# Retention and channel-mix kernel: the values of blocks 1 to 5 computed in 64x64 quarters of the PE array, by couples of head pairs

## The chip, the cores and the metric

The kernel runs on one core of one Trainium2 chip. The metric is the device time of one execution in microseconds (us), lower is better; a time quoted for a kernel is the median of three runs. The engines are named as the profile names them: PE (TensorE), with PEld for its weight loads, DVE (VectorE), ACT (ScalarE), POOL (GpSimd) and SP (SyncE, which here only issues DMAs).

## What is computed

The reference is a retention layer (attention with a decay per head and a running state) followed by a channel-mix layer, all in float32:

```python
# q, k, v: (B=4, H=8, S=768, D=64); lam: (8,)
for b in range(nb):                       # nb = 12 blocks of 64 positions
    intra = (qb @ kb.T * Dmask) @ vb      # Dmask[i, j] = lam ** (i - j) for i >= j
    inter = (qb * lam ** (pos + 1)) @ kv_state
    out[b] = intra + inter
    kv_state = lam ** 64 * kv_state + (kb * lam ** (63 - pos)).T @ vb
x = out as (B, S, 512); x_prev = x shifted by one position
xk = mu_k * x + (1 - mu_k) * x_prev;  xr the same with mu_r
k = relu(xk @ w_k);  v = (k * k) @ w_v;  r = sigmoid(xr @ w_r)
return r * v                              # w_k 512x1024, w_v 1024x512, w_r 512x512
```

## The kernel before

The sequence is cut into six blocks of 128 positions (n = 0 to 5). Every block goes through the same stages. Eight heads make four head pairs, `hp` = 0 to 3; the two heads of a pair (`ab` = 0, 1) lie on the two halves of the 128 partitions. A block has an even and an odd half of 64 positions (`eo` = 0, 1).

- Loads. `load_hp` (L) brings the keys in both layouts, `load_qv` (N) the queries and values. SP issues them. The four input tiles and the `kin` tile have one buffer each, which the next block reuses.
- `scores` (A): keys times queries into the PSUM tile `sc`. For n > 0 each multiplication is 64x64: rows are the head, columns the half. `decay` (a) multiplies the scores on DVE by a table `Dt` of powers of lam into `mv`; `decay_queries` (q) writes the queries times powers of lam into the other 64 partitions of the same `mv`.
- `decay_keys` (k) scales the keys on ACT, `sums` (U) forms keys times values in PSUM tile `u`, `even_state` and `odd_state` (u, w) carry the state `st` forward on DVE. `to_values` copies the state by ACT into the 64 partitions of the value tile that the values leave free.
- `values` (B): one matmul of 128 rows (64 of scores with values, 64 of queries with the state) and 64 columns for each half, batch and head, into PSUM tile `xp`.
- `mix_prev` (e, E), `mix` (f, F) and `split_x` (y, x) form xk and xr and split each into a high and a low part; then the three weight products `r_part` (R, Q), `k_part` (K; in block 0 `k_product`, G) and `v_part` (V), each as three passes of 128x128 by 512 matmuls in a rounded float32 type, with `k_square` (h), `k_split` (p), `r_out` (s) and `v_out` (o) around them.

In block 0 the state is zero, the stages differ in form, and the weights are brought in and converted (S, c, C, D). An unscaled float32 matmul call (scores, sums, values) appears in the trace as two instructions, a rounded one as one.

What sets the order is the string `ORDER`: each three-character step issues its instructions in this sequence on every engine, SP's queue too, and `InOrder` (line 28) keeps the engines from changing it. Waits come from data and from buffers: PSUM has one `sc` pair of banks, one `u` and one `xp` bank, and four banks under the tag `m`, which the weight products, the values and other tiles share. The pool `work` has two `mv` buffers.

The lines that matter here: 114 to 132 (loads), 266 to 350 (scores to `to_values`), 366 to 379 (`values`), 508 on (`ORDER`). The values before:

```python
for eo in range(1 if n == 0 else 2):
    for b in range(B):
        for ab in range(2):
            rows = slice(ab * 64, ab * 64 + 64)
            ...
            tensor.matmul(xp[rows, b, eo, :], vs[eo][:, b, ab, :], mv[:, eo, b, ab, :], start=True, stop=True)
```

Of the kernel before, what the change touches and what calls it, by code (L numbers as in the profile page):

```python
# [18 lines left out]
HP = H // 2  # L19
# [17 lines left out]
def tile_retention_moe(  # L37
# [46 lines left out]
    VS, Q, KT, KN = {}, {}, {}, {}  # L84
# [29 lines left out]
    def load_hp(n, hp):  # L114
        if n == 0:
            return load_first(hp, 0)
        if not KIN:
            KIN.append(const.tile([128, 2, 2, 512], F32, tag="kin", name="kin"))
        t = KIN[0][:, hp % 2]
        views((n, hp), [None, None, None, t[:, 0], t[:, 1]])  # L120
        sync.dma_start(t.rearrange("p c o -> p (c o)"), kk[n - 1, hp])

    def load_qv(n, hp):
        if n == 0:
            return load_first(hp, 1)
        if hp not in QV:
            QV[hp] = const.tile([128, 3, 512], F32, tag=("qv0", "qv1", "wst", "top")[hp], name=f"qv{hp}")
        t = QV[hp]
        views((n, hp), [t[:, 0], t[:, 1], t[:, 2], None, None])
# [4 lines left out]
    smalls = tiny.tile([128, 52 + H], F32, name="smalls")  # L134
# [3 lines left out]
    lows, impulse, ecol, lrow, erow, prow, mus, pair, parity = (smalls[:, a:b] for a, b in (  # L138
        (0, 8), (8, 33), (33, 36), (36, 44), (44, 45), (45, 46), (46, 54), (54, 58), (58, 60)))
# [5 lines left out]
    KD = tiny.tile([128, H], F32, name="KD")  # L145
# [13 lines left out]
    gpsimd.tensor_tensor(KD, lrow, erow.broadcast_to([128, H]), op=ALU.pow)  # L159
# [104 lines left out]
    scs, mvs, us, xps, ts = {}, {}, {}, {}, {}  # L264

    def scores(n, hp):
        q, kt = Q[n, hp], KT[n, hp]
        if n == 0:
            if hp == 1:
# [11 lines left out]
        if (n, hp) not in scs:  # L281
            pair = ps_s.tile([128, 2, 2, B, 64], F32, tag="sc", name="sc")
            scs.update({(n, hp // 2 * 2 + i): pair[:, :, i] for i in range(2)})
        for b in range(B):
            for eo in range(2):
                for ab in range(2):
                    rows = slice(ab * 64, ab * 64 + 64)
                    tensor.matmul(scs[n, hp][eo * 64:eo * 64 + 64, ab, b], kt[rows, b, eo, :], q[rows, b, eo, :],
                                  start=True, stop=True)

    def mv_of(n, hp):
        if (n, hp) not in mvs:
            mvs[n, hp] = work.tile([128, 2, B, 2, 64], F32, tag="mv", name="mv")
        return mvs[n, hp]

    def decay(n, hp):
        sc, mv = scs.pop((n, hp)), mv_of(n, hp)
        if n == 0:
# [3 lines left out]
            return  # L302
        for eo in range(2):
            rows = slice(eo * 64, eo * 64 + 64)

            i = slice(64 - eo * 64, 128 - eo * 64)
            vector.tensor_tensor(
                mv[rows, eo], sc[rows].rearrange("p a b i -> p b a i"),
                Dt[rows, 2 * hp:2 * hp + 2, i].rearrange("p (o a) i -> p o a i", o=1).broadcast_to([64, B, 2, 64]),
                op=ALU.mult)  # L310

    def decay_queries(n, hp):
        q, mv = Q[n, hp], mv_of(n, hp)
        for eo in range(2):
            dr = slice(64, 128) if eo == 0 else slice(0, 64)
            for ab in range(2):
                rows = slice(ab * 64, ab * 64 + 64)
                lp = LP[rows, hp:hp + 1, :].broadcast_to([64, B, 64])
                vector.tensor_tensor(mv[dr, eo, :, ab, :], q[rows, :, eo, :], lp, op=ALU.mult)

    def decay_keys(n, hp):
        kn = KN[n, hp]
        for ab in range(2):
            h = 2 * hp + ab
            scalar.activation(kn[:, :, ab, :], kn[:, :, ab, :], AF.Copy, scale=(PW if n == 0 else KD)[:, h:h + 1])

    def sums(n, hp):
# [8 lines left out]
        if (n, hp, 0) not in us:  # L336
            for eo in halves:
                pair = ps_1.tile([128, 2, B, 64], F32, tag=("u", "xp")[eo], name="u")
                us.update({(n, hp // 2 * 2 + i, eo): pair[:, i] for i in range(2)})
        for b in range(B):  # L340
            for ab in range(2):
                for eo in halves:
                    rows = slice(eo * 64, eo * 64 + 64)
                    tensor.matmul(us[n, hp, eo][ab * 64:ab * 64 + 64, b], kn[rows, b, ab, :], vs[eo][rows, b, ab, :],
                                  start=True, stop=True)


    def to_values(n, hp, eo, x):
        for ab in range(2):
            scalar.copy(VS[n, hp][eo][64 - eo * 64:128 - eo * 64, :, ab, :], x[ab * 64:ab * 64 + 64])  # L350

# [14 lines left out]
    def values(n, hp):  # L366
        mv, vs = mvs.pop((n, hp)), VS[n, hp]
        pool, tag = (ps_1, ("xp", "u")[hp % 2]) if n == 0 else (ps_m, "m")
        xp = pool.tile([128, B, 2, 64], F32, tag=tag, name="xp")
        for eo in range(1 if n == 0 else 2):  # L370
            for b in range(B):
                for ab in range(2):
                    rows = slice(ab * 64, ab * 64 + 64)
                    if n == 0:
                        tensor.matmul(xp[rows, b].rearrange("p e i -> p (e i)"), vs[1][:, b, ab, :], mv[:, ab, b, :], start=True, stop=True)
                    else:
                        tensor.matmul(xp[rows, b, eo, :], vs[eo][:, b, ab, :], mv[:, eo, b, ab, :],
                                      start=True, stop=True)
        xps[n, hp] = xp.rearrange("p b e i -> p b (e i)")

# [101 lines left out]
    def v_out(n, b):  # L482
# [8 lines left out]
        M=lambda n, hp: load_first(hp, 2), b=keep_raw, G=lambda f, hp: k_product(0, f, hp),  # L491
# [17 lines left out]
L00 Z10 L01 M00 M03 T0 k00 Sk4 A00 A01 L02 T2 a00 a01 k03 ck4 M01 B00 A02 Ck4 b00 e00 N01 E00 f00 N02 U00 a02 B01 L03 F00 Dk4  # L509
y00 u00 B02 k01 A03 b01 Sk5 x00 N03 M02 G20 G00 b02 ck5 Sk6 Sk7 E01 a03 G30 Ck5 e01 e02 f01 F01 E02 B03 Dk5 y01 f02 G10 ck6 b03  # L510
U01 Ck6 ck7 k02 Ck7 G11 e03 x01 y02 Sk2 G21 Dk6 G31 f03 U02 u01 Sk3 Dk7 U03 G01 ck2 Ck2 E03 G22 y03 Sr1 ck3 G32 Ck3 G02 G12 G33
Sr0 G23 Sr3 Sv3 Dk2 F02 cr1 Dk3 G13 G03 h03 cr0 Sr2 F03 h02 Cr1 Sv0 h00 cr3 Cr0 N11 Sv1 p01 Dr1 cr2 K07 K05 Dr0 h01 Cr3 Cr2 h05
x02 Dr2 Dr3 x03 K04 p00 h04 u03 Q00 N10 h07 Q01 cv0 Sv2 cv3 u02 q11 Q02 Cv0 Q03 L11 Cv3 Dv0 R00 s03 R01 cv1 Cv1 L10 Dv3 R02 k10
R03 K06 k11 s01 A10 A11 q10 Dv1 cv2 Cv2 U10 L12 p02 h06 U11 Dv2 L13 p03 s02 u11 N13 a10 V04 a11 V02 w11 V03 V05 N12 k13 B11 s00
u10 B10 o01 V00 E11 w10 o02 k12 e11 q13 U13 A12 N20 A13 U12 L20 V06 V01 E10 q12 e10 u12 a12 F11 x11 L21 V07 u13 k20 k21 f10 f11
a13 F10 B13 B12 w13 y10 y11 E13 e13 N21 N22 e12 w12 A20 o03 o00 f12 f13 y12 y13 U21 U20 q21 A21 F13 L22 K10 K11 a20 u20 K13 a21
h11 x13 h10 u21 q20 k22 K14 h13 K12 p10 K15 w20 L23 w21 k23 E12 N23 F12 U22 U23 x10 A23 h12 A22 B20 h15 p11 a23 h14 x12 B21 Q10
E21 L30 e20 L31 Q11 Q12 E20 f20 u22 F20 F21 k31 Q13 s12 s13 q23 K17 h17 K16 N31 e21 N30 R10 h16 R11 R12 p12 u23 w22 x21 k30 p13
x20 V10 V11 f21 R13 w23 s10 a22 V14 V15 q22 o12 B23 E23 B22 y20 U31 U30 A31 A30 s11 y21 e23 L33 o10 V12 N32 u30 f23 y23 e22 V13
V16 F23 u31 f22 q30 x23 E22 F22 y22 o11 V17 K23 h23 o13 w30 x22 K22 K24 L32 q31 Q20 a31 w31 h22 N33 k32 a30 Q21 K25 h24 B31 h25  # L520
B30 k33 U33 q32 N41 e31 E31 F31 A33 U32 A32 f31 Q22 L41 Q23 e30 N40 K26 a32 p22 s22 f30 p21 u33 s23 L40 K20 h26 a33 E30 R20 F30
R21 R22 k40 k41 K21 R23 u32 w32 h20 K27 q33 A40 h21 s21 w33 x30 U41 U40 p20 y30 h27 A41 B33 y31 e33 s20 E33 x31 L43 p23 u40 B32
V22 V24 V25 f33 N43 e32 F33 V23 E32 V20 x33 L42 f32 V21 k42 o21 F32 q40 y32 Q30 a41 w40 o20 x32 a40 Q31 V26 o22 Q32 q41 Q33 s33
y33 V27 K33 k43 N42 o23 u41 K32 w41 K31 s32 h32 B41 B40 h31 N51 A43 e41 h33 E41 U43 f41 e40 p31 A42 L51 F41 a42 E40 U42 K30 h30
a43 R30 L50 K36 R31 q42 h36 R32 f40 k51 u42 F40 u43 K37 R33 s31 h37 K34 s30 K35 k50 q43 B42 x40 p30 h35 p33 h34 w42 N50 N52 B43
A51 y40 U50 U51 p32 y41 A50 E43 x41 e42 V36 V30 L52 V37 F43 e43 N53 f43 a50 o33 f42 V34 x43 V32 y42 V35 E42 o32 V33 a51 q51 y43
# [72 lines left out]
```

## Time and profile before

| | |
|---|---|
| time, median of 3 runs | 396.35 us (395.99 to 396.37) |
| the profiled execution | 395.83 us |
| its span, first to last instruction | 394.0 us |
| PE busy | 387.8 us, 98% of the span |
| DVE, ACT, POOL busy | 244.3, 201.5, 34.4 us |
| granted PE clock | 1.0 of full speed in all 40 slices |

The span lies 1.8 us inside the time of its own execution, and that execution 0.5 us below the median of the runs. Instructions of PE overlap, so the time of a group is read from the chain of waits (start to start), not from its busy time.

### The profile page before, as it was taken

What the parts mean: (1) busy time and instruction counts of PE and PEld (TensorE: products, weight loads), DVE (VectorE), ACT (ScalarE), POOL (GpSimd) and SP (SyncE); (2) the same over time, 40 slices, a digit from 0 to 9 for tenths busy, and PEclk for the clock granted to TensorE, in tenths of its full rate; (3) what the DMA queues carried; (4) which work ended last, traced back from release to release, by engine and by line L of the source; (5) the groups of instructions that cost most, each with busy time, mean ns of one, the idle gap of its engine ahead of it and who ended that gap; (6) DMA issues with size and microseconds to landing.
All of it is one profiled execution on the core that took longest, in us unless ns stands there. A gap on an engine that the chain in (4) does not pass through costs nothing.

```text
span 394.0 us, 8421 instructions
## 1 busy us (share of the span) xinstructions
PE 387.8 (98%) x3532; PEld 321.4 (82%) x3532; DVE 244.3 (62%) x392; ACT 201.5 (51%) x367; POOL 34.4 (9%) x104
## 2 busy tenths in 40 slices
PE   8899999999999999999999999999999999999996
PEld 5777888888888888888888888888888888888886
DVE  6987898699857375876565285855456844222411
ACT  4989997575755362475612347721266542222400
POOL 6540000100110010100100010210000000000000
PEclk9999999999999999999999999999999999999999
DMA  8998934654250081250701070340100001000002
GB/s 302 411 352 300 352 109 137 201 143 166 69 150 0 30 238 57 62 154 0 209 34 57 27 208 8 109 134 27 53 2 2 2 2 55 27 27 2 0 28 80
DMA packets 13606, 42.58 MB, mean 108 GB/s; under 512 B 1920, under 2 KB 2304, under 8 KB 13568
## 3 DMA queue, kind: packets, MB, share of 16 engines
q1 hardware_dynamic: 9824, 35.68, 28.2%
q10 hardware_dynamic: 3744, 6.36, 4.4%
q8 instruction: 28, 0.46, 0.5%
q14 instruction: 10, 0.08, 0.1%
HBM read 35.74 MB, written 6.29 MB: 107 GB/s over the span
## 4 chain that ended last, share of the span: by engine, by line
PE 94%; DVE 1%; POOL 1%; ACT 1%; issue 1%; DMA 0%; POOLq 0%; DVEq 0%
PE vp L33 34%; PE kp L33 32%; PE rp L33 17%; PE xp L33 5%; PE sc L33 3%; PE u L33 3%; POOL lastw L33 1%; PE table L33 0%; DMA smalls<-small 0%; POOL ts L33 0%; ACT ts L33 0%; DVE xl L33 0%; DVE raw L33 0%; POOL pows L33 0%; POOL top L33 0%
## 5 line engine op out<-in xcount | busy, mean ns | idle before, releaser
L33 PE MATMUL vp<-wv,k 128*128 128x512 f32 (+1 forms) x600 | 134.5, 382 | 0.0
L33 PEld LDWEIGHTS vp<-wv,k 128*128 128x128 f32 x600 | 108.9, 188 | 21.9 <-ACT kf L33 0.2
L33 PE MATMUL kp<-xh,wk 128*128 128x512 f32 x384 | 123.3, 391 | 0.0
L33 PEld LDWEIGHTS kp<-xh,wk 128*128 128x128 f32 x384 | 72.1, 188 | 15.7 <-ACT kf L33 0.4
L33 PE MATMUL kp<-xl,wk 128*128 128x512 f32 x192 | 75.0, 390 | 0.0
L33 PE MATMUL rp<-wr,xh 128*128 128x512 f32 x192 | 59.5, 391 | 0.0
L33 DVE TENSOR_TENSOR kf<-kf 128x512 f32<-128x512 f32 x40 | 27.3, 691 | 51.9 <-ACT kf L33 51.7
L33 ACT ACTIVATE kf<-kp 128x512 f32<-128x512 f32 x48 | 28.2, 594 | 54.3 <-PE kp L33 37.8
L33 ACT COPY qv<-st 64x256 f32<-64x256 f32 x80 | 32.4, 405 | 27.4 <-DVE st L33 23.4
L33 DVE TENSOR_TENSOR xl<-ts,xh 128x512 fp32r<-128x512 f32 x48 | 32.5, 688 | 22.0 <-ACT xh L33 21.9
L33 ACT CAST xh<-ts 128x512 fp32r<-128x512 f32 x48 | 29.2, 617 | 28.8 <-DVE rt L33 23.4
L33 PEld LDWEIGHTS kp<-xl,wk 128*128 128x128 f32 x192 | 36.0, 188 | 7.8 <-DVE xl L33 0.6
L33 PEld LDWEIGHTS rp<-wr,xh 128*128 128x128 f32 x192 | 35.8, 188 | 7.5
L33 DVE TENSOR_TENSOR rt<-vp,rt 128x512 f32<-128x512 f32 (+1 forms) x25 | 16.4, 665 | 38.4 <-PE vp L33 38.4
L33 PE MATMUL rp<-wr,xl 128*128 128x512 f32 x96 | 37.4, 390 | 0.0
L33 ACT ACTIVATE ts<-xp,omu 128x512 f32<-128x512 f32 x40 | 26.2, 688 | 18.5 <-PE xp L33 16.9
L33 DVE TENSOR_TENSOR mv<-qv,LP 64x256 f32<-64x256 f32 x80 | 33.6, 421 | 1.5
L33 DVE TENSOR_TENSOR k<-kf,k 128x1024 fp32r<-128x1024 f32 x24 | 29.3, 1225 | 8.1 <-ACT k L33 7.8
L33 DVE SCALAR_TENSOR_TENSOR ts<-xp,smalls,ts 128x512 f32<-128x512 f32 x40 | 29.2, 746 | 7.5 <-ACT ts L33 7.1
L33 DVE TENSOR_TENSOR mv<-sc,Dt 64x512 f32<-64x512 f32 (+1 forms) x48 | 32.5, 686 | 1.1 <-ACT Dt L33 0.5
L33 ACT ACTIVATE rt<-rp 128x512 f32<-128x512 f32 x24 | 14.0, 594 | 30.7 <-PE rp L33 30.7
L33 POOL COPY ts<-lastw 128x4 f32<-128x4 f32 x48 | 15.6, 327 | 138.2 <-DVE xl L33 138.2
(66 smaller groups left out, 294.2 us busy)
## 6 DMA issues: line engine op xcount, KB each, us to landing
qv<-qv SPq DMA_DIRECT2D x40, 256.0 KB, 6.1
kin<-kk SPq DMA_DIRECT2D x20, 512.0 KB, 5.7
out<-rt ACTq DMA_DIRECT2D x23, 256.0 KB, 2.0
raw<-w_v SPq DMA_DIRECT2D x4, 1023.8 KB, 7.2
in<-parts SPq DMA_DIRECT2D x5, 512.0 KB, 5.5
raw<-w_k SPq DMA_DIRECT2D x2, 1023.8 KB, 11.7
raw<-k_half SPq DMA_DIRECT2D x4, 511.8 KB, 8.1
raw<-w_r SPq DMA_DIRECT2D x4, 511.8 KB, 12.2
```

Source lines behind the costliest of these rows:

```text
L33: return lambda *args, **kw: self.tc.keep_in_program_order(op(*args, **kw))
```

## The change

For n > 0 two pairs make a couple (`c` = hp // 2), and the steps L, N, A, a, k, U and B are done for a couple at once. Each pair of a couple gets its own half of the partitions in scores, sums and values. So a score matmul has rows by head and columns by pair, a sum has rows by pair and columns by head, and a value matmul of 128 rows is replaced by two of 64 rows, one of decayed scores with values and one of decayed queries (new tile `qd`) with the state (new tile `SV`), the second added to the first in PSUM. `mv` and `qd` of a couple fill the two `mv` buffers. `Dt` gets a second copy of a table part by POOL (`table`, step d). SP's loads are joined: one DMA of 1 MB where two of 512 KB or four of 256 KB stood. `ORDER` is another order of the steps, the opening included.

```diff
@@ loads
-        t = KIN[0][:, hp % 2]
-        views((n, hp), [None, None, None, t[:, 0], t[:, 1]])
-        sync.dma_start(t.rearrange("p c o -> p (c o)"), kk[n - 1, hp])
+        t = KIN[0].rearrange("p c i o -> p (c i) o")
+        ...
+        sync.dma_start(t.rearrange("p c o -> p (c o)"), kk[n - 1, hp // 2])
...
-            QV[hp] = const.tile([128, 3, 512], F32, tag=("qv0", "qv1", "wst", "top")[hp], name=f"qv{hp}")
-        ...
-        for e in range(2):
-            rows = slice(e * 64, e * 64 + 64)
-            sync.dma_start(t[rows, e:e + 2].rearrange("p c o -> p (c o)"), qv[n - 1, hp, rows])
+            QV[c] = (const.tile([128, 4, 512], F32, tag=("qv0", "wst")[c], name=f"qv{c}"),
+                     const.tile([128, 2, 512], F32, tag=("qv1", "top")[c], name=f"sv{c}"))
+        ...
+        sync.dma_start(t.rearrange("p c o -> p (c o)"), qv[n - 1, c])
@@ scores
-                for ab in range(2):
-                    rows = slice(ab * 64, ab * 64 + 64)
-                    tensor.matmul(scs[n, hp][eo * 64:eo * 64 + 64, ab, b], kt[rows, b, eo, :], q[rows, b, eo, :],
+                for i in range(2):
+                    for ab in range(2):
+                        rows = slice(ab * 64, ab * 64 + 64)
+                        tensor.matmul(sc[i * 64:i * 64 + 64, ab, eo, b], KT[n, hp + i][rows, b, eo, :], Q[n, hp + i][rows, b, eo, :],
@@ table, decay, decay_queries, decay_keys
+    def table(hp):
+        gpsimd.tensor_copy(Dt[64:128, 2 * hp:2 * hp + 2, 64:128], Dt[64:128, 2 * hp + 2:2 * hp + 4, 0:64])
...
         for eo in range(2):
-            rows = slice(eo * 64, eo * 64 + 64)
-            ...
             vector.tensor_tensor(
-                mv[rows, eo], sc[rows].rearrange("p a b i -> p b a i"),
+                mv[:, eo], sc[:, :, eo].rearrange("p a b i -> p b a i"),
...
-                vector.tensor_tensor(mv[dr, eo, :, ab, :], q[rows, :, eo, :], lp, op=ALU.mult)
+            vector.tensor_tensor(qds[n, c][hp % 2 * 64:hp % 2 * 64 + 64, :, :, ab, :], q[rows].rearrange("p b e i -> p e b i"), lp, op=ALU.mult)
...
-            scalar.activation(kn[:, :, ab, :], kn[:, :, ab, :], AF.Copy, scale=(PW if n == 0 else KD)[:, h:h + 1])
+            scale = PW[:, 2 * hp + ab:2 * hp + ab + 1] if n == 0 else KD[:, hp + ab:hp + ab + 1]
+            scalar.activation(kn[:, :, ab, :], kn[:, :, ab, :], AF.Copy, scale=scale)
@@ sums
-            for ab in range(2):
-                for eo in halves:
-                    rows = slice(eo * 64, eo * 64 + 64)
-                    tensor.matmul(us[n, hp, eo][ab * 64:ab * 64 + 64, b], kn[rows, b, ab, :], vs[eo][rows, b, ab, :],
+            for eo in halves:
+                for ab in range(2):
+                    for i, u in enumerate(both):
+                        rows = slice(i * 64, i * 64 + 64)
+                        tensor.matmul(u[ab * 64:ab * 64 + 64, eo, b], kn[rows, eo * B + b, ab, :], vs[eo][rows, b, ab, :],
@@ to_values, values
-            scalar.copy(VS[n, hp][eo][64 - eo * 64:128 - eo * 64, :, ab, :], x[ab * 64:ab * 64 + 64])
+            scalar.copy(SV[n, hp // 2 * 2][eo][i:i + 64, :, ab, :], x[ab * 64:ab * 64 + 64])
...
+        both = [ps_m.tile([128, B, 2, 64], F32, tag="m", name="xp") for _ in range(2)]
+        parts = ((vs, mv), (SV[n, hp], qds[n, hp // 2]))
+        for eo in range(2):
+            for b in range(B):
+                for s, (stay, move) in enumerate(parts):
+                    for ab in range(2):
+                        for i, xp in enumerate(both):
+                            rows = slice(i * 64, i * 64 + 64)
+                            tensor.matmul(xp[ab * 64:ab * 64 + 64, b, eo, :], stay[eo][rows, b, ab, :], move[rows, eo, b, ab, :],
+                                          start=s == 0, stop=s == 1)
@@ ORDER (its first line)
-L00 Z10 L01 M00 M03 T0 k00 Sk4 A00 A01 L02 T2 a00 a01 k03 ck4 M01 B00 A02 Ck4 b00 e00 N01 E00 f00 N02 U00 a02 B01 L03 F00 Dk4
+L00 L01 M03 Z10 T0 A00 A01 k03 T2 M00 Sk4 L02 a00 k00 N01 a01 B00 L03 A02 ck4 b00 B01 Ck4 e00 E00 M02 N02 f00 a02 Sk5 Dk4 y00
```

How the order moves, at three places. First PE in the opening, before (block 0; `sc`, `xp`, `u` are scores, values and sums, `kp` the first weight product):

```order
L33 MATMUL sc<-in 128x128 x8
L33 MATMUL u<-in 64x64 x8
L33 MATMUL xp<-mv,in 64x128 x16
L33 MATMUL sc<-in 128x128 x8
L33 MATMUL kp<-xh_78,wk_265 128x512
```

and in the change, from the same scores of pair 2 on:

```order
L33 MATMUL sc<-in 128x128 x8
L33 MATMUL xp<-mv,in 64x128 x8
L33 MATMUL u<-in 64x64 x8
L33 MATMUL sc<-in 128x128 x8
L33 MATMUL xp<-mv,in 64x128 x8
L33 MATMUL kp<-xh_78,wk_256 128x512
```

The values of pair 1 go ahead of the sums of pair 0, and the values of pair 2 follow the scores of pair 3. Up to the end of the four sums the change issues 18 `kp` matmuls, before 21.

Second, ACT in the opening, before, from the copy of the first values on (`raw<-xp` is that copy, `in` the scaled keys, `st<-u` the copy of a sum):

```order
L33 COPY raw<-xp 128x512
L33 ACTIVATE ts<-raw,omu 128x4x128 x2
L33 CAST wk_265<-raw 128x512
L33 CAST xh_78<-ts 128x512
L33 COPY st_94<-u 128x256
L33 ACTIVATE in<-in,PW 128x4x64 x2
L33 COPY raw<-xp 128x512
L33 CAST xh_82<-ts 128x512
L33 COPY raw<-xp 128x512
L33 ACTIVATE ts<-raw,omu 128x4x128 x4
```

and in the change:

```order
L33 COPY raw<-xp 128x512
L33 ACTIVATE ts<-raw,omu 128x4x128 x2
L33 CAST wk_256<-raw 128x512
L33 CAST xh_78<-ts 128x512
L33 COPY raw<-xp 128x512
L33 COPY st_94<-u 128x256
L33 ACTIVATE ts<-raw,omu 128x4x128 x2
L33 ACTIVATE in<-in,PW 128x4x64 x2
L33 COPY raw<-xp 128x512
L33 CAST xh_82<-ts 128x512
```

After the first cast of `xh` ACT now takes the copy of pair 1's values first, which PE computes after the scores of pair 2. The set of ACT operations up to the first `kf` is the same.

Third, PE at the small matmuls of blocks 1 and 2 that stand ahead of a `vp` or `rp` run, before:

```order
L33 MATMUL u<-qv_817,kin 64x64 x16
L33 MATMUL u<-qv_759,kin 64x64 x16
L33 MATMUL sc<-qv_759,kin 64x64 x16
L33 MATMUL sc<-qv_817,kin 64x64 x16
L33 MATMUL xp<-mv,qv_568 64x64 x16
L33 MATMUL xp<-mv,qv_485 64x64 x16
```

and such a place in the change:

```order
L33 MATMUL sc<-qv_465,kin 64x64 x32
L33 MATMUL u<-qv_465,kin 64x64 x32
L33 MATMUL xp<-mv,qv_812 64x64 x4
L33 MATMUL xp<-qd,sv_813 64x64 x4
L33 MATMUL xp<-mv,qv_812 64x64 x4
L33 MATMUL xp<-qd,sv_813 64x64 x4
```

Sixteen such groups of four make the values of a couple, 64 calls where 32 stood. Counted over blocks 1 to 5, small matmuls break into the weight products 12 times before and 13 times in the change.

## Rows read from the trace of the kernel before

**Rows 1.** The page, busy time by engine and granted clock by slice.

```profile
PE 387.8 (98%) x3532; PEld 321.4 (82%) x3532; DVE 244.3 (62%) x392; ACT 201.5 (51%) x367; POOL 34.4 (9%) x104
PEclk9999999999999999999999999999999999999999
```

**Rows 2.** Chain of waits, opening: start us, us to the next piece, what.

```profile
9.80 0.58 ACT raw L33
...
24.08 0.69 PE u L33 x16
24.76 14.99 PE kp L33 x63
39.76 10.88 PE rp L33 x48
```

**Rows 3.** Chain of waits, blocks 1 to 5.

```profile
53.36 1.09 PE sc L33 x64
54.45 0.93 PE u L33 x64
...
66.55 2.02 PE xp L33 x64
...
103.78 0.93 PE sc L33 x64
104.71 2.02 PE xp L33 x64
106.73 5.69 PE rp L33 x24
112.42 5.44 PE kp L33 x24
...
251.26 0.62 PE sc L33 x32
251.88 0.85 PE u L33 x29
```

**Rows 4.** Chain of waits, the end.

```profile
368.84 22.08 PE vp L33 x120
...
390.95 0.42 DVE rt L33
```

**Rows 5.** Timeline of PE, opening; in brackets the idle time before and what ended it.

```profile
10.98 1.16 PE L33 MATMUL sc<-in 64*128 64x128 f32 x16 [1.27 <-DMA in<-parts]
12.07 0.69 PE L33 MATMUL u<-in 128*64 128x64 f32 x16
24.08 0.69 PE L33 MATMUL u<-in 128*64 128x64 f32 x16 [0.71 <-ACT st L33]
```

**Rows 6.** Timeline of ACT, opening.

```profile
12.16 0.61 ACT L33 CAST xh<-ts 128x512 fp32r<-128x512 f32 x1
23.13 0.62 ACT L33 CAST wk<-raw 128x512 fp32r<-128x512 f32 x1 [1.00 <-DVE raw L33]
23.66 0.37 ACT L33 COPY st<-u 128x256 f32<-128x256 f32 x1
30.64 0.59 ACT L33 ACTIVATE kf<-kp 128x512 f32<-128x512 f32 x1
```

**Rows 7.** Groups by form, DVE and ACT: busy us, mean ns, idle before.

```profile
L33 DVE TENSOR_TENSOR mv<-sc,Dt 64x512 f32<-64x512 f32 x40 | 27.4, 686 | 0.4
L33 DVE TENSOR_TENSOR mv<-qv,LP 64x256 f32<-64x256 f32 x80 | 33.6, 421 | 1.5
L33 ACT ACTIVATE kin<-kin,KD 128x256 f32<-128x256 f32 x40 | 17.9, 503 | 1.8 <-DMA kin<-kk 1.6
```

**Rows 8.** DMA issues: what, how many, KB each, median us to landing.

```profile
kin<-kk SPq DMA_DIRECT2D x20, 512.0 KB, 5.7
raw<-w_v SPq DMA_DIRECT2D x4, 1023.8 KB, 7.2
raw<-w_r SPq DMA_DIRECT2D x4, 511.8 KB, 12.2
```

More of the change, by code (lines that the diff above doesn't have):

```diff
@@ L83, in tile_retention_moe @@
     KIN, QV = [], {}
-    VS, Q, KT, KN = {}, {}, {}, {}
+    VS, SV, Q, KT, KN = {}, {}, {}, {}, {}
     def views(key, parts):
@@ L280, in scores @@
             return
-        if (n, hp) not in scs:
-            pair = ps_s.tile([128, 2, 2, B, 64], F32, tag="sc", name="sc")
-            scs.update({(n, hp // 2 * 2 + i): pair[:, :, i] for i in range(2)})
+        scs[n, hp] = sc = ps_s.tile([128, 2, 2, B, 64], F32, tag="sc", name="sc")
         for b in range(B):
             for eo in range(2):
-                for ab in range(2):
-                    rows = slice(ab * 64, ab * 64 + 64)
-                    tensor.matmul(scs[n, hp][eo * 64:eo * 64 + 64, ab, b], kt[rows, b, eo, :], q[rows, b, eo, :],
[L289 to L294, printed above, removed]
+                for i in range(2):
+                    for ab in range(2):
+                        rows = slice(ab * 64, ab * 64 + 64)
+                        tensor.matmul(sc[i * 64:i * 64 + 64, ab, eo, b], KT[n, hp + i][rows, b, eo, :], Q[n, hp + i][rows, b, eo, :],
+                                      start=True, stop=True)
+    def table(hp):
+        gpsimd.tensor_copy(Dt[64:128, 2 * hp:2 * hp + 2, 64:128], Dt[64:128, 2 * hp + 2:2 * hp + 4, 0:64])
     def decay(n, hp):
-        sc, mv = scs.pop((n, hp)), mv_of(n, hp)
+        sc = scs.pop((n, hp))
+        mv = work.tile([128, 2, B, 2, 64], F32, tag="mv", name="mv")
         if n == 0:
@@ L335, in sums @@
         halves = range(2 if n + 1 < NT else 1)
-        if (n, hp, 0) not in us:
+        both = [ps_1.tile([128, 2, B, 64], F32, tag=tag, name="u") for tag in ("u", "xp")]
+        us.update({(n, hp + i, eo): u[:, eo] for i, u in enumerate(both) for eo in range(2)})
+        for b in range(B):
             for eo in halves:
[L338 to L341, printed above, removed]
-                for eo in halves:
-                    rows = slice(eo * 64, eo * 64 + 64)
-                    tensor.matmul(us[n, hp, eo][ab * 64:ab * 64 + 64, b], kn[rows, b, ab, :], vs[eo][rows, b, ab, :],
-                                  start=True, stop=True)
+                for ab in range(2):
+                    for i, u in enumerate(both):
+                        rows = slice(i * 64, i * 64 + 64)
+                        tensor.matmul(u[ab * 64:ab * 64 + 64, eo, b], kn[rows, eo * B + b, ab, :], vs[eo][rows, b, ab, :],
+                                      start=True, stop=True)
     def to_values(n, hp, eo, x):
+        i = hp % 2 * 64
         for ab in range(2):
-            scalar.copy(VS[n, hp][eo][64 - eo * 64:128 - eo * 64, :, ab, :], x[ab * 64:ab * 64 + 64])
+            scalar.copy(SV[n, hp // 2 * 2][eo][i:i + 64, :, ab, :], x[ab * 64:ab * 64 + 64])
     def even_state(n, hp):
@@ L367, in values @@
         mv, vs = mvs.pop((n, hp)), VS[n, hp]
-        pool, tag = (ps_1, ("xp", "u")[hp % 2]) if n == 0 else (ps_m, "m")
-        xp = pool.tile([128, B, 2, 64], F32, tag=tag, name="xp")
-        for eo in range(1 if n == 0 else 2):
+        if n == 0:
+            xp = ps_1.tile([128, B, 2, 64], F32, tag=("xp", "u")[hp % 2], name="xp")
             for b in range(B):
@@ L373, in values @@
                     rows = slice(ab * 64, ab * 64 + 64)
[L374 to L379, printed above, removed]
+                    tensor.matmul(xp[rows, b].rearrange("p e i -> p (e i)"), vs[1][:, b, ab, :], mv[:, ab, b, :], start=True, stop=True)
+            xps[n, hp] = xp.rearrange("p b e i -> p b (e i)")
+            return
+        both = [ps_m.tile([128, B, 2, 64], F32, tag="m", name="xp") for _ in range(2)]
+        parts = ((vs, mv), (SV[n, hp], qds[n, hp // 2]))
+        for eo in range(2):
+            for b in range(B):
+                for s, (stay, move) in enumerate(parts):
+                    for ab in range(2):
+                        for i, xp in enumerate(both):
+                            rows = slice(i * 64, i * 64 + 64)
+                            tensor.matmul(xp[ab * 64:ab * 64 + 64, b, eo, :], stay[eo][rows, b, ab, :], move[rows, eo, b, ab, :],
+                                          start=s == 0, stop=s == 1)
+        for i, xp in enumerate(both):
+            xps[n, hp + i] = xp.rearrange("p b e i -> p b (e i)")
     raws = {}
@@ L563 @@
         "parts": np.concatenate([inputs[hp, :, a:b].reshape(-1) for hp in range(HP) for a, b in zip(CUTS[hp], CUTS[hp][1:])]),
-        "kk": np.concatenate([x[1:] for x in blocked[2:]], axis=3),
-        "qv": np.concatenate([
-            np.concatenate([blocked[i][1:, :, rows] for i in order], axis=3)
-            for rows, order in ((slice(0, 64), (1, 0)), (slice(64, 128), (0, 1)))], axis=2),
+        "kk": np.concatenate([two(blocked[2]), couples(reverse(cut(k)))], axis=3),
+        "qv": np.concatenate([two(blocked[0]), couples(reverse(cut(v)))], axis=3),
         "small": np.concatenate([
```

89 lines of the change are left out of this document (48 added, 41 removed).

## The prediction

> **What bounds the kernel now.** [...] A busy PE need not be a PE that does useful work, so the chain of waits is read next. From 24.08 us on it consists of PE pieces alone, up to the last matmul, whose end a short DVE multiplication and its output DMA follow [rows 2, 4]. So DVE and ACT set the end nowhere behind the opening; what counts there is how long PE takes for its list. The rate of that list: 24 matmuls of 512 columns take 5.44 us, 0.2267 each [rows 3]. The last 120 pieces and what follows them are the same in the change, so the tail costs nothing either way.
>
> In the opening, PE waits. The timeline shows three waits: 1.27 us for the scores' load of pair 2, 0.71 us before the last two sums, for ACT's copy of a sum [rows 5], and one that the chain hides: 63 `kp` matmuls take 14.99 us where 63 x 0.2267 + 0.25 (entering the big shape, below) is 14.53, so 0.46 us of waiting is inside [rows 2, 3].
>
> **The change, part by part.**
>
> *Values in quarters.* A couple's values are 32 calls now, 64 instructions, in 2.02 us; in the change they are 128 instructions of 64 rows by 64 columns. Such instructions exist: 64 of scores in four quarters take 0.93 us, 14.5 ns each [rows 3]. 128 x 14.5 = 1.86 us. The piece of 2.02 us holds an entry cost as well: the first small group behind a weight product takes 1.09, the second 0.93, so changing the shape costs 0.16 [rows 3]; 2.02 - 0.16 = 1.86. Twice the instructions at half the price: the work itself gains 0. The upper bound for an accumulating quarter, which no row shows, is the 29.1 ns that a value matmul takes now (1.86 / 64); I take 14.5, since scores and sums have the same shape, rows and columns.
>
> [...]
>
> *Shape changes.* Values of 64 columns by 128 rows are another shape than the sums and scores of 64 by 64: values behind scores take the same 2.02 us as values behind a weight product [rows 3], so 0.16 us is paid there too. The order of PE before has eight places where values stand beside scores or sums within one interruption of the weight products. In the change all three have one shape: 8 x 0.16 = 1.28 us less. Bounds: 0, if a quarter that accumulates counts as another shape, and 1.28.
>
> *Interruptions.* Going back costs too: 24 matmuls behind values take 5.69 us instead of 5.44, 0.25 [rows 3]. There are 13 interruptions instead of 12: 0.16 + 0.25 = 0.41 us more.
>
> *Sums of block 5.* Here only the even half is wanted. Before, rows are the half, so two of four quarters stand empty: 29 instructions in 0.85 us, 29 ns each [rows 3]. In the change rows are the pair and all four work. 64 instructions x 14.5 ns = 0.93 us less.
>
> *The opening.* The wait of 1.27 us stays: ahead of that load stand the same DMAs in another order. The 0.71 goes, by this schedule. From 9.80 us (copy of the first values) to 30.64 us (first `kf`) ACT is idle for 1.00 us, waiting for the third piece of the weights, which POOL and then DVE prepare [rows 2, 6]. In the change POOL does that piece between the second and the third use of its small copies, and ACT comes to it with over a microsecond to spare; in exchange ACT now wants pair 1's values at 12.77 us [rows 6], which PE has only behind the scores of pair 2, at about 13.3 (12.07 [rows 5] and 16 matmuls more). So 20.84 - 1.00 + 0.6 = 20.4 us, and the first `kf` at 30.3. ACT's copy of pair 1's sum started at 23.66 [rows 6]; in the change the idle 1.00 goes, the 0.6 comes, and two casts of 0.53 that stood ahead of it stand behind it: 22.2. PE starts that sum at about 20.9, when its keys are scaled, then does three `kp` matmuls and pair 2's sum and asks for the copy's buffer at about 22.9: no wait. `kp` matmuls follow with all their operands, so the 0.46 goes also. Together 1.17; I take 1.1, as PE has a small new wait before the sum of pair 1, whose keys ACT scales late. Ends: 0 or slightly below, if each wait comes back in another place, and 1.2.
>
> *DVE, ACT, POOL, SP.* Decay halves: 20 multiplications over 128 partitions for 40 over 64, 686 ns each, 13.7 us less work. The decayed queries: 80 x 421 ns become 40 of twice the columns, between 421 and 842 each; by the nearest form, 686, 6.2 us less. Scaled keys: 40 x 503 ns become 20 [rows 7], at most twice as long, so 0 to 10 us less. All of it lies beside PE work and is worth 0; it is margin for waits. POOL's two table copies stand in the opening, ahead of the weight products of block 0, and are first used by block 1, which began at 53.36 [rows 3]. SP issues fewer, larger DMAs; their landing counts only where the next block waits (below).
>
> *Sum*: -1.1 - 1.28 + 0.41 - 0.93 = -2.9 us. Against the profiled execution: 395.83 - 2.9 = 392.9. It was 0.5 below the median of the runs, which is what I forecast: 396.35 - 2.9 = **393.4 us**.
>
> **The rivals.**
>
> *The opening gives nothing.* ACT and POOL run one after the other there, so a delay of any of them moves PE; the order was altered from its first line on. For it: ACT is without idle time both ways. Against it: the three waits of PE are known and two have slack. Then only -1.28 + 0.41 - 0.93 remains: 394.5 us. Still faster.
>
> *A wait eats the gain.* `mv` and `qd` of a couple fill the pool's two buffers, so the next couple's multiplications start only behind the values that read them. The closest pair is in block 1: between the two values stand 48 big matmuls and a group of sums and scores, 48 x 0.2267 + 2.02 + 0.5 = 13.4 us. The change's DVE list there, four `qd` and two `mv` (6 x 0.69), four state updates and some eight others of 0.69, makes about 9.5 us. Slack 4 us, but operations that wait for ACT stand in it. If it costs what is gained, about 396.2 us, no change.
>
> *Slower: a couple's load comes late.* Keys have one buffer of 1 MB, and its load starts behind the couple's sums and scores. The shortest time to the next scores is from block 1's second couple to block 2's first: 36 x 0.2267 + 0.25 + 2.02 = 10.4 us. A 512 KB load of keys lands in 5.7 us, a 1 MB load of weights in 7.2, loads in a full queue in 12.2 [rows 8]. Behind it ACT scales the keys (1.0 to 1.4 us), in front of other ACT work, and the sums wait. It decides from about 9 us of landing; with 12.2 PE stands for some 3 us there, and ACT, held meanwhile, passes on as much to the next values: 396.35 - 2.9 + 2 x 3.2 = 399.8 us. Against it: DMA traffic is low at that time, and everywhere else 12 to 30 us are left.
>
> *Quarters that do not overlap when they accumulate.* Two instruction series now add up in one PSUM place, 8 instructions apart; no small matmul of the trace does that between calls. By rows the worst is 29.1 ns: 1280 x 14.6 = 18.7 us more, 412.1 us; it is slower from 2.9 ns more per instruction on, counting the margin of measurement. Against it: each call is already two instructions on one place. [...]
>
> That the change is not what it says can be left out: PE's order shows the quarters, and no other matmul goes or comes.
>
> **How the numbers follow.** A measurement of this kernel tells about 0.2%, 0.8 us, from no change. Forecast 0.60; opening without gain 0.14; both faster, 0.74. A wait that eats the gain 0.11: same. Late loads 0.10 and quarters that do not overlap 0.05: slower, 0.15. The range: below, 0.8 to 1 us of gain that I may have missed in the opening (the 1.27), 392.4; above, up to the edge of the eaten gain, 396.6, which leaves out the slower cases and about 0.05 below.
>
> **What would show it.** Right: values of a couple in 1.86 us, 2.02 where they come first; sums of block 5 in 0.47 a couple; no wait of PE before the last two sums of block 0; the third big product (`rp`) starting near 38.7 instead of 39.76 us; PE's pieces unbroken to the end, the last matmul done near 388.0 instead of 390.93. Wrong: a PE wait for `mv`, `kin` or `qv` in blocks 1 to 5, above all before the scores of block 2; values of over 2.1 us; the last sums of block 0 later than 24 us.

## The result, and the profile after

The change takes 399.58 us (median of 6 runs, 398.77 to 401.28) where the kernel before takes 396.38 beside it (395.99 to 397.75): a ratio of 1.0085, 95% interval 1.0059 to 1.0111. It is slower by 3.2 us; 393.4 was forecast, and the range ended at 396.6. The profiled execution is the slowest of the six, 401.28 us; a second one, taken later, is 398.78. Both are read here, the second wherever sizes matter. One execution of all those told of below, the profiled one of the second cut, took 484.56 us at a mean granted clock of 0.753; it is left out of that kernel's time, and that kernel has no chain to show.

The page of the change, to be read against [rows 1], and the line of the instruction queue, which the kernel before has as "28, 0.46, 0.5%":

```profile
PE 388.8 (97%) x4172; PEld 321.9 (81%) x4172; DVE 222.9 (56%) x332; ACT 199.1 (50%) x347; POOL 32.4 (8%) x106
PEclk9899999999999999999999999999999999999999
...
q8 instruction: 33, 0.54, 0.6%
```

PE has 640 matmuls and 640 weight loads more, DVE 21 us less to do. The bound is still PE, but its pieces no longer run without a break. The chain of waits of the same execution (start us, us to the next piece, what), with what answers to [rows 2 to 4]:

```profile
41.51 5.44 PE rp L33 x24
...
55.11 1.09 PE sc L33 x64
...
68.25 2.02 PE xp L33 x128
...
102.44 1.87 PE xp L33 x128
...
127.10 1.86 PE xp L33 x125
128.96 1.49 issue
130.45 0.33 PE xp L33 x2
...
154.80 0.45 PE sc L33 x29
155.25 1.37 issue
156.62 0.74 PE sc L33 x34
...
259.81 0.47 PE u L33 x30
...
290.43 0.62 PE u L33 x32
291.06 1.87 PE xp L33 x128
...
293.03 1.51 issue
294.55 1.08 PE sc L33 x57
...
374.29 22.08 PE vp L33 x120
...
396.40 0.42 DVE rt L33
```

Three pieces are "issue": PE stands in the middle of a group of small matmuls and waits for nothing that the profile shows. The kernel before has no such piece of more than 0.02 us behind 24.08 us. Together they are 4.37 us here and 2.67 in the second profile:

```profile
54.15 1.09 PE sc L33 x64
...
128.18 0.87 issue
...
153.84 0.85 issue
...
291.12 0.95 issue
...
393.88 0.02 issue
```

This gives the account of the second profile against the profiled execution of before, 398.78 - 395.83 = 2.95 us. The first scores of block 1 start at 54.15 instead of 53.36 [rows 3]: 0.79 in the opening. From there to the last matmul's end it takes 393.88 - 54.15 = 339.73 where it took 390.93 - 53.36 = 337.57 [rows 3, 4]: 2.16. What follows is the same.

The opening of the first profile shows the other thing that the forecast did not have, in the timeline of PE and in a table by stretch (us, then busy time of PE, PEld, DVE, ACT and POOL, granted clock, DMA share, GB/s):

```profile
11.83 1.52 PE L33 MATMUL sc<-in 64*128 64x128 f32 x14 [1.74 <-DMA in<-parts]
```

```profile
10.00:12.25 2.25, 0.51 (x9) 0.45 (x9) 0.95 (x2) 2.10 (x5) 1.51 (x4) 1.00 1.02 408
12.25:15.66 3.41, 3.41 (x38) 3.19 (x36) 2.46 (x5) 1.16 (x3) 0.64 (x2) 0.50 1.06 412
...
```

PE waited 1.74 us for the load of pair 2, and behind that its granted clock was 0.50 of full speed for 3.41 us, with 1.00 before and after. The second profile has no such stretch behind its wait of 1.50:

```profile
11.13 1.16 PE L33 MATMUL sc<-in 64*128 64x128 f32 x16 [1.50 <-DMA in<-parts]
```

The first scores of block 1 start 0.96 us later in the first profile. Of that 0.70 is the load (11.83 instead of 11.13), and 0.26 is left for the clock. Such a fall is not the change's alone: beside one of the experiments, three of nine executions of the kernel before have a mean clock of 0.994 to 0.996, where the others have 0.999 or 1.0. So it is not what makes the median slower.

### The profile page after: what moved, and what is told of

It reads as the page before. It is cut to its first block, busy times and chain, and to the rows that moved or that the text cites. A ratio compares the mean times of both kernels' runs of the same rounds, so it can differ in the third digit from the quotient of the medians.

```text
span 399.5 us, 9519 instructions
## 1 busy us (share of the span) xinstructions
PE 388.8 (97%) x4172; PEld 321.9 (81%) x4172; DVE 222.9 (56%) x332; ACT 199.1 (50%) x347; POOL 32.4 (8%) x106
## 2 busy tenths in 40 slices
DMA packets 10409, 42.65 MB, mean 107 GB/s; under 512 B 1280, under 2 KB 1664, under 8 KB 7808
## 4 chain that ended last, share of the span: by engine, by line
PE 95%; DMA 2%; issue 1%; SPq 1%; DVE 0%
PE vp L33 33%; PE kp L33 33%; PE rp L33 16%; PE xp L33 6%; PE sc L33 3%; PE u L33 3%; DMA in<-parts 2%; SPq L33 1%; DVE rt L33 0%
## 5 line engine op out<-in xcount | busy, mean ns | idle before, releaser
L33 ACT COPY sv<-st 64x256 f32<-64x256 f32 x80 | 32.3, 404 | 23.5 <-DVE st L33 22.6
L33 ACT CAST k<-kf 128x1024 fp32r<-128x1024 f32 x24 | 25.0, 1049 | 9.0 <-DVE kf L33 7.2
L33 DVE TENSOR_TENSOR qd<-qv,LP 64x512 f32<-64x512 f32 x40 | 27.4, 685 | 3.1 <-PE xp L33 2.5
L33 DVE SCALAR_TENSOR_TENSOR st<-st,LC,u 128x256 f32<-128x256 f32 x36 | 16.9, 476 | 12.5 <-ACT sv L33 12.3
```

The lines of the kernel that those rows point to most:

```text
L33: return lambda *args, **kw: self.tc.keep_in_program_order(op(*args, **kw))
```

## The experiments

Two questions: what are the three breaks, and why did the opening not get shorter. Theory A: PE's own instructions reach the core as packets, and a packet comes too late where too many small instructions stand in a row; the rival (B) looks for the cause in the work at the three places. Theory C: the changed order of the opening costs time; theory D: only the landing of pair 2's load does. The place in the list where a new packet begins is called a boundary below. For A the clue is the q8 line: 5 packets more for 1280 more PE instructions, so 256 to a packet; and, counted in the trace from 0 and with PE's semaphore instructions, the breaks stand before PE's instructions number 3521, 4033 and 7105, whose distances (512 and 3072) are multiples of 256. The transfers in a window around the second break, 153.7 to 155.5 us, hold one packet of that queue; from 136 to 153.7 us there is none:

```profile
q8 instruction: 1, 0.02, 4.8%
```

**The boundaries moved, in the change.** The scores of block 1's first couple are issued twice (128 instructions more, into the same place), which leaves all work at the three places as it was.

```diff
-        for b in range(B):
+        for b in range(2 * B if (n, hp) == (1, 0) else B):
+            b = b % B
```

> The change with the scores of block 1's first couple issued twice (the second time over the first, same values): 64 more small matmuls, 128 more PE instructions, 0.93 us of PE work; everything behind them is shifted by half a packet of 256 instructions. Theory A (PE's instructions come in packets of 16 KB, 256 instructions; the three breaks of 1.4 to 1.5 us in the change all stand before PE instruction 193 + 256 k; a packet is asked for when the one before is entered and is usable some 4.0 us later, so a run of 512 small instructions, 3.9 us, outruns it when a boundary falls late in the run): the breaks leave the values of block 2 (129 us), the scores of block 3 (155 us) and of block 5 (293 us) or move within those runs, and others appear; with the boundaries half a packet earlier six of the seven long runs hold one late, 1.6 us each, together about 10 us instead of 4.4, so about 6 to 7 us slower than the change, near 406 us. Theory B (the breaks belong to those matmuls: a wait for a buffer or data that the profile does not name): the same three breaks before the same matmuls, time 0.9 us above the change, near 400.5 us.

Measured: 406.40 us (405.93 to 407.12), 1.0243 of before (1.0225 to 1.0261). The old breaks are gone from their places and six stand elsewhere, as theory A had it, also in the time. Chain of waits:

```profile
87.42 1.55 issue
...
130.68 1.47 issue
...
158.85 1.44 issue
...
197.17 1.16 issue
...
232.57 0.91 issue
...
265.22 0.86 issue
```

They stand before instructions 2241, 3521, 4289, 5057, 5825 and 6593: again all apart by multiples of 256, at the same remainder as the three. The same work breaks or not by where it falls in the count. Theory A holds; what the work is does not decide.

**The boundaries moved, in the kernel before.** The scores of block 1's first pair issued twice (64 instructions).

```diff
-        for b in range(B):
+        for b in range(2 * B if (n, hp) == (1, 0) else B):
+            b = b % B
```

> The kernel before with the scores of block 1's pair 0 issued twice: 32 more small matmuls, 64 more PE instructions, 0.47 us of PE work, everything behind shifted by a quarter of a packet. Theory A: the kernel before has runs of 384 small instructions too, values at 29 ns each in them, so slower in instructions; its packet boundaries happen to fall well. With the shift four runs hold a boundary late (before the scores or sums near 86 us, 106, 167 and 189 us), with breaks of 0.8 to 1.0 us each: 3.9 us and 0.5 of work, about 400.7 us. Theory B: no break, 396.8 us.

Measured: 401.05 us (400.17 to 401.52), 1.0102 of before (1.0083 to 1.012); the scores themselves account for 0.47 of its 4.4 us (1.56 instead of 1.09 [rows 3]). Chain of waits:

```profile
54.04 1.56 PE sc L33 x96
...
107.08 0.53 issue
...
168.85 1.91 issue
...
193.62 0.56 issue
...
236.45 0.21 issue
```

The large one stands before instruction 3777, at the same remainder of 256 as all others. The time is as theory A expected, the sizes are not: one long break and three short ones, where four of 0.8 to 1.0 us were expected. So the kernel before, too, can have these breaks; that it has none depends on where its boundaries lie.

**The long runs cut, first try.** Big matmuls put into the three runs, nothing more or less computed (in the order: first the step, then block and pair; V12 and V14 are parts of the third product, Q40 and Q41 of the second; from here on the lines of a diff are the pieces of `ORDER` lines that matter).

```diff
-U30 B22 q30 V12 e23
+U30 V12 B22 q30 e23
-B30 A32 k32 U32 V14 q32
+B30 V14 A32 k32 U32 q32
-B50 A52 Q40 Q41 E51
+B50 Q40 Q41 A52 E51
```

> The change with three steps of 12 big matmuls moved into the three runs of small matmuls in which PE breaks off: V12 between sums and values in block 2, V14 between values and scores in block 3, Q40 and Q41 between values and scores in block 5. No instruction more or less. Theory A: big matmuls take 15 times as long per instruction, so the packets arrive in time: all three breaks go, 4.4 us and some 0.8 us of slow starts behind them; three more interruptions cost 0.41 each; 4.0 us less than the change, about 395.5 us. Theory B: the breaks stay at their matmuls or come elsewhere, time 1.2 us above the change, about 400.8 us.

Measured: 398.92 us (398.44 to 399.17), 1.0052 of before (1.0038 to 1.0066). The breaks are gone, the time hardly moves: a wait of 1.47 us from start to start has come at 141.61, in a k product of block 2. Timeline of PE:

```profile
143.09 0.50 PE L33 MATMUL kp<-xh,wk 128*128 128x512 f32 x1 [1.08 <-ACT xh L33]
```

V12 no longer stands between block 2's values and this product, and the split `xh` of those values, which ACT casts at 142.41, comes too late. (The expectation of the next cut calls this a PSUM wait; by the profile it is one for an operand.) Theory A is right about the breaks here; the price of the cut is not yet known.

**The opening's order of before, first try.** The steps of the opening in the order of before, with the load step Sv1 of w_v in the place of a later one.

```diff
-L00 L01 M03 Z10 T0 A00 A01 k03 T2 M00 Sk4 L02
+L00 Z10 L01 M00 M03 T0 k00 Sk4 A00 A01 L02 T2
...
-F02 cr1 Sv1 G32
+Sr0 G23 Sr3 Sv1
```

> The change with the opening of the kernel before: the steps of block 0 up to its second k_square stand in the order of before, the loads too. Theory C (the opening loses time through its order: the load of pair 2 lands 0.9 us later and the gap of 2.0 us that this leaves on PE lets the clock fall to half for 3.4 us): the load lands near 10.8 us, the gap is 1.5 us, no fall of the clock, the first rp product starts near 39.8 us instead of 41.5 in the profile; the time 1 to 2 us below the change, about 398 us. Rival D (landing and clock vary from run to run and the order has no part in it): rp starts within 0.5 us of 41.5 less what the clock took (1.5), i.e. near 40, in either order, and the medians are within 0.5 us. The three breaks later on stay in either case.

Measured: 405.66 us (404.68 to 406.31), 1.0221 of before (1.0201 to 1.0241). A miss, and of no use for theories C and D: the edit put a load of w_r behind one of w_v that waits for its place. Its chain of waits shows the step, 7.69 us for that load, and the three breaks (1.48, 1.16 and 1.37 us) at their places in the list, 5 to 7 us later:

```profile
33.06 7.69 DMA raw<-w_r
```

**The runs cut another way.** Twelve r matmuls in place of V12, so that V12 stays behind the values; the other two cuts as above.

```diff
-x21 R13 Q13 p10 s11 s13 w22 w23 A30 s10 p11 U30 B22
+x21 w22 w23 A30 U30 R13 Q13 p10 s11 s13 s10 p11 B22
-B30 A32 k32 U32 V14 q32
+B30 V14 A32 k32 U32 q32
-B50 A52 Q40 Q41 E51
+B50 Q40 Q41 A52 E51
```

> The change with its longest runs of small matmuls cut, and no instruction more or less: twelve rp matmuls that stood before block 2's sums now stand between block 3's first scores and block 2's values (the two score splits and the state step ahead of them come earlier by as much); as in the second experiment, 16 v matmuls stand between block 2's values and block 3's second scores and two r groups between block 4's values and the sums of block 5. The v matmuls that moved in the second experiment stay behind block 2's values. Theory A (a packet of 256 PE instructions is asked for too late when over some 320 small ones run in a row): all three breaks of PE are gone, 1.49 + 1.37 + 1.51 = 4.4 us, three more interruptions cost 3 x 0.41 = 1.2; without the PSUM wait of 1.47 us of the second experiment the time is 3 to 3.5 us below the change, about 396. Rival (the breaks come from something else, or turn into waits for PSUM or for the states): within 0.8 us of the change, breaks or waits of 1 us and more still in the chain.

Measured: 398.68 us (397.72 to 399.15), 1.0057 of before (1.0042 to 1.0072). A miss by 2.7 us; the run with both edits, further down, has the same cuts and shows why.

**The opening's order of before, without the fault.** The load step Sv1 stands behind the last one of w_r.

```diff
-L00 L01 M03 Z10 T0 A00 A01 k03 T2 M00 Sk4 L02
+L00 Z10 L01 M00 M03 T0 k00 Sk4 A00 A01 L02 T2
...
-Ck3 Dk2 G02 F02 cr1 Sv1 G32 G33
+cr0 Sr2 Sv1 N10 F03 h02
```

> The change with the opening's order of before, as far as the changed program has the same steps; the one v copy comes right behind the third r copy, so that no load of w_r stands behind a load of w_v that waits (which spoiled the third experiment), and the table copies stand behind the last states. Theory C (the changed order of the opening costs time: ACT wants pair 1's values before PE has them, and waits 2.2 us): the rp matmuls start near 40.4 us where pair 2's load lands near 11.5 and near 39.8 where it lands near 10.8, instead of 41.0 and later; all behind them as in the change, three breaks too; 0.6 to 1.5 us below the change, 398 to 399. Theory D (only the landing of the load and the clock that falls behind it made the opening later): within 0.4 us of the change.

Measured: 399.58 us (398.83 to 400.59), 1.0084 of before (1.0065 to 1.0104); three breaks. The change, unaltered, beside it:

> The change itself, unaltered, on the chip of the three runs beside it, for a second profile. Theory A: PE's breaks stand at the same three instructions again (block 2's values, the scores of blocks 3 and 5), each 1.3 to 1.6 us. Theory D: where the load of pair 2 lands below 11.3 us and the granted clock does not fall in the opening, the rp matmuls start by 40.2 us; theory C: at 40.8 or later even so. Time 399 to 400 us.

Measured: 399.87 us (398.78 to 400.80), 1.009 of before (1.0072 to 1.0107), the breaks at the same three instructions, but of 0.85 to 0.95 us only. The two medians are 0.3 us apart, as theory D has it. The profiles say otherwise: with the order of before the first scores of block 1 start at 54.02, with the changed order at 54.15, although pair 2's load had landed 0.3 us earlier there (its scores start at 11.13 instead of 11.44). So the order costs time, less than theory C expected; the table further down has all runs.

**Both.** The two last edits together.

> The two edits of the experiments run beside it, the cut runs and the opening's order of before. If theories A and C hold, their gains add, as they lie in different stretches: 3 to 3.5 and 0.6 to 1.5 us below the change, 394.5 to 396, which is 0.5 to 2 us below the kernel before. If one of them falls, 396 or over.

Measured: 398.35 us (398.13 to 398.39), 1.0051 of before (1.0039 to 1.0063). A miss, and its waits of PE say why (us in total, times, longest):

```profile
PE u L33 <- DVE st L33: 1.1, 1, 1.1
...
PE u L33 <- ACT st L33: 0.7, 1, 0.7
PE xp L33 <- ACT rt L33: 0.4, 1, 0.4
```

No break behind the opening, but two waits that the cut made, the first and the third (the second, of the opening, is the 0.71 of [rows 5], back with the order of before). Block 3's sums come 2.7 us earlier, and the state steps of block 2, which free their PSUM, stand on DVE behind three x splits (1.90 us). And block 2's values now follow the last r matmuls at once, and want PSUM that ACT is still copying out.

**The same with the two waits taken out.** The state steps ahead of the x splits on DVE, the r steps s (ACT) partly behind the values; PE's order is untouched.

```diff
-y20 x20 k30 Q12 R12 x21 w22 w23 A30 U30 R13 Q13 p10 s11 s13 s10 p11 B22 q30
+w22 w23 y20 x20 k30 Q12 R12 x21 A30 U30 R13 s11 s10 Q13 p10 p11 B22 s13 q30
```

> The run with both edits, with the two waits that the cut of block 2's run brought taken out: the odd state steps stand ahead of three x splits on DVE, so that PE need not wait for them at block 3's first sums (1.05 us), and one of the gate copies of r (ACT) ahead of the last six rp matmuls, another behind block 2's values, so that the PSUM of the values is free in time (0.65 us). PE's order is the same to the instruction. Theory A: no break of PE is left, the last matmul ends 1.0 to 1.7 us earlier than in the run with both edits, 396.5 to 397.3 us; that is 2.5 to 3 us below the change with one and the same work, and level with the kernel before. Rival (what the breaks gave back always returns as a wait elsewhere): 398 or more.

Measured: 396.33 us (396.00 to 397.92, 12 runs), 1.001 of before (0.9997 to 1.0023). With the same work and the same number of matmuls the time is 3.0 to 3.3 us below the change, each against the kernel before beside it. The rival, that the gain always comes back as a wait elsewhere, falls.

**The three cuts alone, and with the opening of before, side by side.** The first is the change with only the edits of the last two diffs and the two other cuts; the second is the kernel just told of.

> The change with the three cuts of the run before this one and nothing else: the opening is the change's own again. Theory A: no break of PE, the time 2.7 to 3.5 us below the change (399.6 to 399.9 so far), that is 396.2 to 397.1. Against the same kernel with the opening's order of before, run beside it: theory C (the changed order costs time) 0.3 to 0.8 us more, theory D (only the landing of pair 2's load sets the opening) within 0.2, and what the prediction said of the opening (its order saves 1.1 us) 1.1 less, 395.2.

> The run before this one again, unaltered, on the chip of the run beside it: the three cuts and the opening's order of before. 396 to 396.7 us, level with the kernel before; it is there to be compared with the run beside it.

Measured: the cuts alone 396.82 us (395.59 to 397.73, 12 runs), 1.0008 of before (0.9995 to 1.0021); with the opening of before 396.41 (396.00 to 397.00, 12 runs), 0.9994 (0.9981 to 1.0008). The chain of waits of the cuts alone from the first scores of block 1 to the end, with the one stop that is left (pieces on the way to V12, for whose PSUM ACT copies; PE itself stands 0.2 us for it):

```profile
54.36 1.09 PE sc L33 x64
...
125.64 0.59 ACT rt L33
...
127.06 1.06 ACT k L33
...
391.70 0.42 DVE rt L33
```

Three cuts are worth 2.8 to 3.1 us to the change and bring it level with the kernel before. No version beats the kernel before by more than a measurement can tell.

By these medians the order of the opening is worth 0.4 us, inside what the runs scatter. The profiles separate it from the load. Between the scores of pair 2, which start as their load lands, and the first scores of block 1 stands the part of the opening that the order changes (us; the profiles with an undisturbed opening, as one with a fallen clock or a late load of w_r would mix in something else):

| profile | scores of pair 2 | first scores of block 1 | between |
|---|---|---|---|
| the kernel before | 10.98 | 53.36 | 42.38 |
| the same, boundaries moved | 11.69 | 54.04 | 42.35 |
| changed order: the change, second profile | 11.13 | 54.15 | 43.02 |
| changed order: the cuts alone | 11.35 | 54.36 | 43.01 |
| changed order: boundaries moved | 11.67 | 54.68 | 43.01 |
| changed order: runs cut, first try | 11.66 | 54.65 | 42.99 |
| order of before: without the fault | 11.44 | 54.02 | 42.58 |
| order of before: both | 11.48 | 54.04 | 42.56 |
| order of before: two waits taken out | 11.47 | 54.04 | 42.57 |
| order of before: the same again | 11.75 | 54.31 | 42.56 |

The rows of the last line, from the timeline of PE and the chain of waits:

```profile
11.75 1.16 PE L33 MATMUL sc<-in 64*128 64x128 f32 x16 [2.13 <-DMA in<-parts]
```

```profile
54.31 1.09 PE sc L33 x64
```

So the changed order costs 0.44 us whatever the load does (theory C, within the 0.3 to 0.8 of its last expectation), and the load moves the start of block 1 by up to 0.8 us from run to run (theory D); both are at work. The 0.2 us between the order of before in the changed program and in the kernel before is not explained.

## Why the prediction was wrong

**The step that failed: "Twice the instructions at half the price: the work itself gains 0."** The price was right: a couple's values take 1.87 us, and 2.02 where they come first, as forecast, also where quarters add up in one PSUM place. But the step, and the rivals too, priced an instruction only by its time on PE, and took it that the list is always there. 640 more matmuls are 1280 more instructions and 5 more packets, and the change also does a couple's scores, sums and values in runs of up to 512 instructions (384 in the kernel before). Of those PE takes 256 in 1.87 us. Where it broke off in the first profile, it passed the boundary 3.62, 3.50 and 3.61 us after the one before, so a long run can outpace its supply. From the packet's landing to PE's next instruction another 1.42 to 1.58 us passed there (at the second break 155.19 to 156.62).

How far ahead the packet is asked for is not seen in a row. An estimate from the first profile: at its three breaks the boundary was passed 4.07 to 4.69 us after PE began the 320th instruction ahead of it, while 320 small ones take 320 x 0.93 / 128 = 2.3 us. The boundaries without a break bear it out: in that profile and in the one of before, behind the opening, none was passed sooner than 3.90 us after the 320th, while some were passed without a break 1.87 us after the 256th, so the packet is asked for earlier than that (its transfer begins up to 297 instructions ahead in these two; 310 or 340 would fit as well as 320). So a break stands where a boundary falls near the end of a long run (0.2 to 1.9 us of "issue" in these runs), and in the two profiles none of over 0.3 us from start to start was seen where more than three large matmuls stood among the 320.

Three breaks are few for this change: in the run that moved the boundaries by 128 instructions there were six.

**The sizes.** The cuts alone show what the body is worth without breaks: 391.68 - 54.36 = 337.32 us against 337.57, so -0.25. By the prediction's terms it is -1.28 + 0.41 - 0.93 = -1.8, with three more interruptions (3 x 0.41 = 1.23) and the 0.2 of the stop above -0.37. So these terms hold to 0.1 us, all together: shape changes, interruptions, sums of block 5 (0.47 and 0.62 a couple). The body of the change in the second profile, +2.16, is then -1.8 and 3.96 for the breaks: 2.67 in the three "issue" pieces; most of the rest is slow starts behind them, 0.8 (in the first profile two matmuls in 0.33 us at 130.45), and two smaller stops, 0.4 (at 84.69 and 227.27).

**The opening: -1.1 forecast, +0.79 in the second profile.** What was said of ACT's first wait is right: it wants pair 1's values 0.7 us too early. But "In the change POOL does that piece between the second and the third use of its small copies, and ACT comes to it with over a microsecond to spare" failed. Timeline of ACT, second profile, for [rows 6]:

```profile
13.36 0.59 ACT L33 COPY raw<-xp 128x512 f32<-128x512 f32 x1 [0.71 <-PE xp L33]
...
21.89 0.62 ACT L33 CAST wk<-raw 128x512 fp32r<-128x512 f32 x1 [0.47 <-DVE raw L33]
...
23.73 1.14 ACT L33 CAST xh<-ts 128x512 fp32r<-128x512 f32 x2 [0.95 <-POOL ts L33]
...
31.45 0.58 ACT L33 ACTIVATE kf<-kp 128x512 f32<-128x512 f32 x1
```

and of POOL and PE:

```profile
21.84 1.31 POOL L33 CAST top<-raw 128x512 f16<-128x512 bf16 x1
23.07 0.63 POOL L33 COPY ts<-lastw 128x4 f32<-128x4 f32 x1
```

```profile
25.60 0.50 PE L33 MATMUL kp<-xl,wk 128*128 128x512 f32 x1 [0.69 <-DVE xl L33]
```

The wait for the weights shrinks from 1.00 to 0.47 us, and ACT waits 0.95 for POOL's `ts`, a small copy that POOL begins only at 23.07, behind another cast of the weights (`top`, 1.31 us). ACT is idle for 2.13 us instead of 1.00; the first `kf` comes at 31.45 instead of 30.64, where 30.3 was forecast. On PE the 0.71 before the last two sums is gone, and 0.69 for a late x split stands before a `kp`. That is the mechanism of the rival "the opening gives nothing", which allowed for no loss. By the table above the opening of the change costs 0.64 us (43.02 against 42.38), 0.44 of it by its order; the other 0.15 of the 0.79 is the load of pair 2, which lands when it will: PE waited 1.27 us for it before, 1.21 to 2.13 us since, so the 1.27 that "stays" was never one number.

**In sum**: the opening is off by 0.79 + 1.1 = 1.89 us, the breaks are 3.96, and 1.89 + 3.96 = 5.85 is the distance between +2.95 and -2.9.

**What held beside.** No wait of PE for `mv`, `qd`, `kin` or `qv` in blocks 1 to 5, so two rivals (full buffers, a couple's load late) did not happen; decay takes 684 ns over 128 partitions, a decayed query 685, scaled keys 715, inside their bounds, and DVE's 21 us less changed nothing, as forecast. One thing stays open: why the breaks of one and the same kernel last 0.87, 0.85 and 0.95 us in one execution and 1.49, 1.37 and 1.51 in another. In the one with the longer breaks the transfer of the three packets took 0.88, 1.38 and 1.46 us, and that of its other packets 0.89 to 1.63; what sets it is not shown.

## What to carry to other kernels

Price a small instruction twice: by its time on the engine, and by its place in the engine's list; where a change halves the size of the instructions and doubles their number, look at the instruction queue's packets and at the longest run without a large instruction. A dozen large matmuls in such a run cost 0.41 us here and saved a break of 0.9 to 1.5, if the waits that the new order makes are taken out too. And where one unchanged place runs well and the next does not, add a few instructions far ahead of both: if the breaks move with the count, as here, where three became six at other places, it is the supply.

## What was not expected of the hardware

- PE's instructions come as packets of 256 during the execution (28 packets of that queue before, 33 with 1280 instructions more), and a break of mostly 0.85 to 1.9 us stands where one comes late; the profile calls it "issue" and names no cause.
- The number of such breaks goes with the position in the count: three in the change, six when 128 instructions are put ahead; none in the kernel before, and one of 1.91 us with three small ones when 64 are put ahead.
- The granted clock fell to 0.50 of full speed for 3.41 us behind a wait of 1.74 us in the opening of one execution. In the openings with waits of 1.50 and 1.90 us it stayed at 1.00, and the execution with a wait of 2.13 us has a mean of 0.999.
- The load of pair 2 let its scores start between 10.98 and 11.75 us in the profiles of the table, and the start of block 1 moved with it, to 0.03 us, in either order.
